# An expert layer whose order is planned by a list scheduler in the source: every instruction pinned, products chained in PSUM, output sums in DRAM

## The chip, the cores and the metric

One core of a Trainium2 chip runs the whole kernel. The metric is device time in microseconds (us) of one execution, lower is better; three executions of the kernel before were timed. Engine names are those of the profile: PE multiplies matrices and PEld loads its weights beside it, DVE, ACT and POOL work on elements, SP issues most DMAs.

## What is computed

Block-sparse attention (batch 4, 8 heads, 768 positions, head size 64) gives x, 3072 rows of 512. A gate x @ w_gate (8 experts) is turned into weights P by eight rounds of row and column normalisation. Every expert then works on every row, with no routing:

```python
for e in range(E):                    # E = 8, D = 512, F = 1024
    h = np.maximum(x @ w1[e], 0.0)
    ye = h @ w2[e]
    out += P[:, e:e + 1] * ye
```

Both products are large and dense: the expert part is 32 pairs of (expert, batch of 768 rows).

## The kernel before

**Two parts.** The attention part is planned in steps T (`at`, L270): the loop at L927 sorts the work of each step and hands it to `in_order` (L917), which chains every instruction to the one made before it on the same engine, so each engine keeps the source's order. Its last steps hold: the values of the last tile (T = 194), the preparation of expert 0's w2 (`start_w2`, L897: a 2 MB load, eight ACT parts at L108, DVE `whole` at L194, a PE transpose `spread` at L114, DVE `power`), and `turn_x` (L793, T = 196 and 197: PE transposes at L798, ACT copies at L805). The expert part that follows isn't chained to it: its instructions are placed by the framework's own scheduler, which may put them before attention instructions made earlier; only side work is held behind its place (`not_earlier`, L983).

**Expert part.** For i = 4e + b, `stage1` (L1199) computes h = relu(x @ w1) and `stage2` (L1312) h @ w2. Each operand is a high and a low fp16 half, so one term takes three matmuls. Both stages use seven products of half-size blocks in place of eight (p = 0 to 6). Stage one has four quarters `qi` per i. A quarter's product (L1208) is six matmuls of 384 columns into one PSUM bank of its own; bank by bank, DVE adds it to running sums in SBUF (`comb`, L1220, seven per quarter), ACT copies the first (L1255), applies relu (L1259, L1275, L1279, L1287) and writes the high half of h (L1230); the low half is a subtraction on POOL for p = 2, 3, 5 and on DVE for the rest (L1234, L1240). POOL makes four sums (L1282, L1094). Stage two has seven products by three row blocks `ci`; each group is twelve matmuls of 256 columns (L1333), read by DVE into `acc` (L1357), for expert 0 in part by ACT (L1354). The output sums `acc` of all four batches stay in SBUF; the last expert's are stored at L1363, one row block and half at a time. While i is in stage two, i + 1 is in stage one: the main loop alternates products of the one with quarters of the other.

**Side work.** New weights of each expert pass once through one raw buffer: load (L177), eight ACT parts (L108), splits into halves on ACT (L1072) and DVE (L1076), block sums on POOL (L1087). A `Slots` queue (L996) with hand-set costs and due times spreads this over the main loop. Expert 0's splits, the last batch's x (`finish_x`, L346) and the gate's rounds (`balance`, L1152) fall into the first rounds of the expert part. x is loaded per product, in 384 KB pieces (L227).

Of the kernel before, what the change touches and what calls it, by code (L numbers as in the profile page):

```python
# [24 lines left out]
TOP = 2.0 ** 12  # L25
# [4 lines left out]
HDOWN = 2.0 ** -20  # L30
HUP = 2.0 ** 20
# [9 lines left out]
PRE, LB2, LB1 = 0, 1, 1  # L41
PIN = 0
TW = 100
TF = 146
HQ = 300
NHA = 10
LATE = 40
# [3 lines left out]
LAV = 3  # L51


@with_exitstack
def tile_sparse_attention_moe(
# [79 lines left out]
    def scale_power(tag, s, inv):  # L135
# [6 lines left out]
        nc.vector.tensor_scalar(s, s, TOP, None, ALU.mult)  # L142
        nc.vector.tensor_scalar(inv, a, 1.0 / TOP, None, ALU.mult)

# [35 lines left out]
    def scale_steps(which, e, vector=nc.vector, scalar=nc.scalar):  # L180
# [18 lines left out]
        def power():  # L199
            vector.tensor_reduce(out=a, in_=wr["all", which], axis=AX.X, op=ALU.max)  # L200
            vector.tensor_scalar(a, a, TINY, HUGE, ALU.max, ALU.min)
            ai = a.bitcast(I32)
            vector.tensor_scalar(ai, ai, 0x7F800000, None, ALU.bitwise_and)
            vector.reciprocal(s, a)
            vector.tensor_scalar(s, s, TOP, None, ALU.mult)
            vector.tensor_scalar(inv, a, 1.0 / TOP, None, ALU.mult)

# [138 lines left out]
    def finish_x(b):  # L346
        xf = xfs.pop(b).rearrange("p k c t -> p k (c t)")
        quad = {
            (j, k): xf[:, j * KH : (j + 1) * KH, k * TH : (k + 1) * TH]
            for j in range(2) for k in range(2)  # L350
        }

        def split(src, p, nm):
            st = xst.tile([P, 2, KH, TH], F16, tag="xs", name=f"xs_{b}_{nm}")
            nc.scalar.activation(st[:, 0], src, AF.Copy)
            nc.vector.tensor_tensor(out=st[:, 1], in0=src, in1=st[:, 0], op=ALU.subtract)
            if p is not None:
                nc.sync.dma_start(out=xd[b][:, p], in_=st)
            return st

        def plain(k):
            sts = [
                split(quad[j, k], {(0, 0): 0, (1, 0): 1, (1, 1): 2}.get((j, k)), f"b{j}{k}")
                for j in range(2)
            ]
            ps = bank[0](f"lg_{b}_{k}")
            for i in range(CH):
                for kc in range(KD):
                    for m, (l, w) in enumerate(((1, gh), (0, gl), (0, gh))):
                        nc.tensor.matmul(  # L370
                            ps[:, i * NE : (i + 1) * NE],
                            lhsT=sts[kc // KH][:, l, kc % KH, i * P : (i + 1) * P],
                            rhs=w[:, kc],
                            start=(kc == 0 and m == 0), stop=(kc == KD - 1 and m == 2),
                        )
            t0 = b * NC + k * CH
            nc.vector.tensor_scalar(
                lg[:, t0 : t0 + CH].rearrange("p t e -> p (t e)"), ps[:, : CH * NE],
                inv_v[:, b : b + 1], inv_g, ALU.mult, ALU.mult,
            )  # L380

        def diff(nm, x, y, out, p):
            nc.gpsimd.tensor_tensor(out=out, in0=x, in1=y, op=ALU.subtract)
            split(out, p, nm)

        x00, x01, x10, x11 = (quad[j, k] for j in range(2) for k in range(2))
        return [
            lambda: plain(0),
            lambda: plain(1),
            lambda: diff("t1", x01, x00, x00, 4),  # L390
            lambda: diff("t3", x11, x01, x01, 6),
            lambda: diff("t2", x11, x00, x00, 5),
            lambda: diff("t4", x10, x00, x10, 3),
        ]

    with ExitStack() as actx:
# [18 lines left out]
        plan = xfp.tile([P, 2, S], BF16, tag="xf", name="plan")  # L415
        onehot = plan[:, 0]
# [148 lines left out]
        def scale_v(b):  # L565
            sv[b] = small.tile([P, 1], F32, tag="sv", name=f"sv_{b}")
            scale_power(f"v{b}", sv[b], inv_v[:, b : b + 1])
# [246 lines left out]
        def split_gate():  # L814
            scale_power("g", sg, inv_g)
# [116 lines left out]
        xlast = finish_x(B - 1)  # L932

    class InOrder:
        def __init__(self, engine):
            self.engine = engine

        def __getattr__(self, name):
            call = getattr(self.engine, name)
            if not PIN:  # L940
                return call
            return lambda *a, **kw: tc.keep_in_program_order(call(*a, **kw))

    class Pinned:
        vector, scalar, gpsimd = (InOrder(x) for x in (nc.vector, nc.scalar, nc.gpsimd))
# [3 lines left out]
    )  # L949
    sk = mpool("sk", 1)  # L950
    upool = mpool("upool", NU)
    hA = mpool("hA", 1)
    hB = mpool("hB", 1)
    big = mpool("big", 1)
    def spare(n):
        return sk.tile([P, n], F32, name=f"spare_{next(count)}")

    count = iter(range(99))
    ps_h = mpool("ps_h", 4, space=PSUM)
    ps_y = mpool("ps_y", 4, space=PSUM)  # L960

    DH = DM // 2
    w2p = [big.tile([P, 2, KF // 2, DH], F16, name=f"w2p_{p}") for p in range(NP)]
    hfree = [
        (hA if n < NHA else hB).tile([P, 2, TH], F16, name=f"h_{n}") for n in range(NHT)
    ]
    accs = {b: big.tile([P, NC, DM], F32, name=f"acc_{b}") for b in range(B // 2)}
    bank[0] = lambda nm: ps_y.tile([P, 512], F32, tag="py", name=nm)
    spread_bank[0] = lambda nm: ps_h.tile([P, 512], F32, tag="ph", name=nm)

    def acc(t):
        return accs[t // NC][:, t % NC]

    def finish_late():
        slots.need(("late", 0, 0))
        late.close()
        right = mpool("right", 1, side="right")
        for b in range(B // 2, B):
            accs[b] = right.tile([P, NC, DM], F32, name=f"acc_{b}")

    aside = set()

    def not_earlier(fn):  # L983
        made = nc.cur_bb.bb.instructions
        n = len(made)
        fn()
        for ins in list(made[n:]):
            if ins.engine not in SIDE:
                continue
            for old in reversed(made[:n]):  # L990
                if old.engine == ins.engine and old.name not in aside:
                    tc.add_manual_dep(ins, old.name, behind, reason="not_ahead_of_its_place")
                    break
            aside.add(ins.name)

    class Slots:  # L996
        def __init__(self):
            self.now, self.pe, self.busy = 0, 0.0, [0.0, 0.0, 0.0]
            self.urgent, self.lazy = [], []
            self.last = 0  # L1000

        def add(self, fn, key, delay=1, lazy=False, dve=0.0, act=0.0, pool=0.0, gap=0):
            queue = self.lazy if lazy else self.urgent
            queue.append((fn, key, self.now + delay, (dve, act, pool), gap))

        def charge(self, costs):
            self.busy = [x + c for x, c in zip(self.busy, costs)]

        def run(self, queue, n):
            fn, key, _, costs, _ = queue.pop(n)  # L1010
            self.charge(costs)
            if queue is self.lazy:
                self.last = self.now
            if key[0] in ("scale", "w1", "w2"):
                not_earlier(fn)
            else:
                fn()

        def fits(self, costs):
            return all(  # L1020
                not c or x <= self.pe + lead
                for x, c, lead in zip(self.busy, costs, LEADS)
            )

        def tick(self, pe, dve, act=0.0):
            self.now += 1
            self.pe += pe
            self.busy = [max(x, self.pe - lag) for x, lag in zip(self.busy, LAGS)]
            self.charge((dve, act, 0.0))
            n, held = 0, set()  # L1030
            while n < len(self.urgent):
                _, key, ready, costs, _ = self.urgent[n]
                if key not in held and ready <= self.now and self.fits(costs):
                    self.run(self.urgent, n)
                    n, held = 0, set()
                    continue
                held.add(key)
                if key[0][0] == "sum":
# [358 lines left out]
    for i in range(NI):  # L1397
# [35 lines left out]
        if last:  # L1433
            parts[1]()
# [43 lines left out]
```

## Time and profile before

| | |
|---|---|
| three executions | 2235.66, 2236.8 (median), 2239.47 us |
| profiled execution, first to last instruction (span) | 2232.8 us |
| PE busy | 2162.7 us, 97% |
| DVE, ACT, POOL busy | 75%, 58%, 63% |
| first expert matmul | 414.07 us into the span |

The span is of one more execution than the three; its own time outside the span is not listed, so the span is read beside the median, which is 4.0 us longer. "Busy" of PE is the union of matmul rows whose ends are modelled, so a busy PE need not be a PE at its full rate; the rate is read from how many matmuls a stretch holds.

### The profile page before, as it was taken

What the parts mean: (1) busy time and instruction counts of PE and PEld (TensorE: products, weight loads), DVE (VectorE), ACT (ScalarE), POOL (GpSimd) and SP (SyncE); (2) the same over time, 40 slices, a digit from 0 to 9 for tenths busy, and PEclk for the clock granted to TensorE, in tenths of its full rate; (3) what the DMA queues carried; (4) which work ended last, traced back from release to release, by engine and by line L of the source; (5) the groups of instructions that cost most, each with busy time, mean ns of one, the idle gap of its engine ahead of it and who ended that gap; (6) DMA issues with size and microseconds to landing.
All of it is one profiled execution on the core that took longest, in us unless ns stands there. A gap on an engine that the chain in (4) does not pass through costs nothing.

```text
span 2232.8 us, 47313 instructions
## 1 busy us (share of the span) xinstructions
PE 2162.7 (97%) x18892; PEld 1596.3 (71%) x18892; DVE 1671.7 (75%) x2927; ACT 1285.1 (58%) x2393; POOL 1412.6 (63%) x1481
## 2 busy tenths in 40 slices
PE   6999999889999999999999999999999999999999
PEld 4777766566777777777777777777677767776777
DVE  8888888778778767866786678667866786678664
ACT  5788888754566546554555455545554555455442
POOL 5556678685568555855685658565856585658553
PEclk9999999999999999999999999999999999999999
DMA  7766965312121212121212121212121212121221
GB/s 167 151 154 138 209 146 126 130 69 88 51 88 50 88 50 88 50 89 50 88 50 88 50 88 50 89 50 88 50 88 50 88 51 88 51 88 58 79 79 51
DMA packets 195347, 192.36 MB, mean 86 GB/s; under 512 B 132125, under 2 KB 150581, under 8 KB 195125
## 3 DMA queue, kind: packets, MB, share of 16 engines
q1 hardware_dynamic: 194560, 189.30, 29.3%
q8 instruction: 148, 2.42, 0.5%
q14 instruction: 75, 0.61, 0.1%
q10 hardware_dynamic: 564, 0.03, 0.0%
HBM read 140.54 MB, written 17.30 MB: 71 GB/s over the span
## 4 chain that ended last, share of the span: by engine, by line
PE 64%; DVE 11%; POOL 9%; ACT 7%; issue 4%; DMA 4%; DVEq 0%; SPq 0%; POOLq 0%; ACTq 0%
PE py L1333 26%; PE p L1208 25%; PE u L767 3%; DMA r<-in_moe_w_dram 3%; PE m L669 2%; PE m L672 2%; PE t L702 2%; PE t L705 2%; ACT h L1230 2%; POOL r L1087 2%; ACT unread L108 2%; POOL s L1282 2%; POOL h L1240 1%; DVE attic L1076 1%; POOL r L1094 1%
## 5 line engine op out<-in xcount | busy, mean ns | idle before, releaser
L1333 PE MATMUL py<-w2p,h 128*128 128x256 f16 x8064 | 952.4, 273 | 12.2 <-ACT acc L1354 4.2
L1333 PEld LDWEIGHTS <-h 128*128 128x128 f16 x8064 | 787.7, 98 | 154.0 <-issue 16.6
L1240 POOL TENSOR_TENSOR h<-u,h 128x384 f16<-128x384 f32 x128 | 124.4, 972 | 558.8 <-ACT h L1230 541.4
L1208 PEld LDWEIGHTS <-attic 128*128 128x128 f16 x3072 | 299.5, 98 | 202.2 <-issue 20.5
L1208 PE MATMUL p<-attic 128*128 128x384 f16 x2304 | 412.0, 326 | 12.7 <-DVE a L1220 8.0
L1208 PE MATMUL p<-arena 128*128 128x384 f16 x2304 | 415.3, 326 | 5.9 <-DVE u L1220 2.7
L1357 DVE SCALAR_TENSOR_TENSOR acc<-py,spare,acc 128x256 f32<-128x256 f32 (+1 forms) x588 | 295.0, 514 | 145.3 <-PE py L1333 143.2
L1208 PEld LDWEIGHTS <-arena 128*128 128x128 f16 x2304 | 225.2, 98 | 134.1 <-issue 7.8
L1230 ACT ACTIVATE h<-c 128x384 f16<-128x384 f32 x256 | 132.5, 520 | 319.9 <-DVE c L1220 263.0
L1220 DVE SCALAR_TENSOR_TENSOR a<-p,a 128x384 f32<-128x384 f32 x384 | 211.2, 550 | 22.7 <-PE p L1208 16.6
L678 DVE TENSOR_REDUCE top<-m 128x1 f32<-128x768 f32 x192 | 181.7, 951 | 46.7 <-PE m L672 45.8
L710 ACT ACTIVATE pe<-t,qk 128x768 int32<-128x768 f32 x192 | 172.3, 899 | 68.7 <-PE t L705 60.3
L1230 ACT ACTIVATE h<-s 128x384 f16<-128x384 f32 x128 | 66.8, 522 | 174.3 <-POOL s L1282 174.2
L1230 ACT ACTIVATE h<-r 128x384 f16<-128x384 f32 x256 | 131.3, 519 | 61.3 <-POOL r L1094 58.3
L1240 DVE TENSOR_TENSOR h<-s,h 128x384 f16<-128x384 f32 x128 | 106.2, 830 | 79.5 <-ACT h L1230 79.3
L1094 POOL TENSOR_TENSOR r<-s,r 128x384 f32<-128x384 f32 x128 | 153.6, 1200 | 10.0
L1094 POOL TENSOR_TENSOR c<-c,r 128x384 f32<-128x384 f32 x128 | 151.1, 1180 | 10.0
L1282 POOL TENSOR_TENSOR s<-a,u 128x384 f32<-128x384 f32 x128 | 140.9, 1101 | 17.3 <-ACT a L1279 17.1
L1208 PE MATMUL p<-arena,attic 128*128 128x384 f16 x768 | 146.2, 326 | 5.4 <-ACT a L1255 4.7
L1240 POOL TENSOR_TENSOR h<-r,h 128x384 f16<-128x384 f32 x128 | 133.9, 1046 | 18.3 <-ACT h L1230 15.2
L724 POOL TENSOR_SCALAR pl<-pe 128x768 f16<-128x768 uint16 x112 | 96.3, 864 | 70.9 <-ACT pe L710 68.8
L1087 POOL TENSOR_TENSOR r<-r 128x256 f32<-128x256 f32 (+1 forms) x106 | 119.0, 1148 | 31.0 <-DVE arena L1076 31.0
(206 smaller groups left out, 3717.3 us busy)
## 6 DMA issues: line engine op xcount, KB each, us to landing
arena<-xd SPq DMA_DIRECT2D x128, 384.0 KB, 3.9
attic<-xd SPq DMA_DIRECT2D x96, 384.0 KB, 4.2
r<-in_moe_w_dram SPq DMA_DIRECT2D x16, 2048.0 KB, 8.7
arena<-in_q_dram SPq DMA_DIRECT2D x16, 384.0 KB, 4.3
arena<-in_k_dram SPq DMA_DIRECT2D x16, 384.0 KB, 4.7
arena<-in_v_dram SPq DMA_DIRECT2D x4, 1536.0 KB, 7.8
xd<-xs_t SPq DMA_DIRECT2D x16, 384.0 KB, 2.9
out_dram<-acc SPq DMA_DIRECT2D x48, 128.0 KB, 1.7
```

The lines of the kernel that those rows point to most:

```text
L678: nc.vector.tensor_reduce(out=tops[n][:, c : c + 1], in_=sc[:, :S], axis=AX.X, op=ALU.max)
L710: nc.scalar.activation(pe, sc[:, :S], AF.Exp, bias=EXP_SHIFT, scale=qk[n // 2][3])
L724: nc.gpsimd.tensor_scalar(lo, low, FINE, 1.0, ALU.mult, ALU.mult)
L1087: lambda c=c: Pinned.gpsimd.tensor_tensor(out=out[:, c], in0=x[:, c], in1=y[:, c], op=op),
L1094: nc.gpsimd.tensor_tensor(out=out, in0=x, in1=y, op=ALU.subtract)
L1208: nc.tensor.matmul(ps, lhsT=w1p[p][:, l, kc, fs], rhs=xp[p][:, r, kc], start=(kc == 0 and m == 0), stop=(kc == KH - 1 and m == 2),)
L1220: nc.vector.scalar_tensor_tensor(out=t, in0=ps, scalar=HDOWN, in1=other, op0=ALU.mult, op1=ALU.add)
L1230: nc.scalar.activation(h[:, 0], src, AF.Relu if relu else AF.Copy)
L1240: eng.tensor_tensor(out=h[:, 1], in0=src, in1=h[:, 0], op=ALU.subtract)
L1282: nc.gpsimd.tensor_tensor(out=s1, in0=a1, in1=u3, op=ALU.add)
L1333: nc.tensor.matmul(py, lhsT=hs[i, p, kc][:, l, tsl], rhs=w2p[p][:, r, kc], start=(old is None and kc == 0 and m == 0), stop=(kc == KF // 2 ...
L1357: nc.vector.scalar_tensor_tensor(out=dst, in0=src, scalar=c, in1=dst, op0=ALU.mult, op1=ALU.add)
```

## The change

The expert part is rewritten. Each operation becomes a `Job` with its engine, a cost in us written in the source, its dependencies and the buffers that it takes and gives back. `Plan.run` lists the jobs by a simulation in the source: PE takes, of the jobs that are ready, the one planned earliest; DVE, ACT and POOL take the one with the earliest due time; times other than PE's are raised by 6%, and 0.2 us lies between engines. The resulting order goes through `in_order`, so it is chained on every engine, behind the attention part.

Stage one now works on two quarters at a time. Products 0, 5, 4, 2 add up in one PSUM bank per quarter and 6, 3 in another; between two products of a chain the running sum is read out (ACT three times and once more with relu, DVE three times per quarter). The low halves of p = 0, 2, 3, 4, 5, 6 go to DVE or POOL, whichever the plan finds free sooner. The output sums live in DRAM between experts (`accd`): two pieces of 768 KB per i are loaded and stored, through three buffers in SBUF; the last expert stores four pieces of 384 KB per i to the output. x pieces, weights and their splits are the same work, ordered by the plan. With `TWO = ()` the code for a second level of block products is present but makes no instruction. The scale constants change by powers of two. Matmul shapes and counts of both stages are unchanged.

```diff
 EPS = 1e-9
-NHT = 30
-NU = 8
-LOP = (2, 3)
-LOPE = (2, 3, 5)
-NLE = 99
-LEADS, LAGS = (1.0, 1.0, 1.0), (1.0, 1.0, 1.0)
-SD = (2, 3, 4, 5)
+TWO = ()
+NB1, NH, NPAIRS, NU, NACC = 4, 28, 8, 8, 3
+SLK, SLK2, SHIFT, EASE = 1.5, 2.0, 8.0, 0.3
...
+class Plan:
+    LAT = 0.2
+    DMA_RATE, DMA_LAND = 190.0, 2.0
+    MARGIN = 1.06
...
+                    if e == "PE":
+                        best = min(ok, key=lambda j: (j.pt is not None, j.pt if j.pt is not None else j.seq))
+                    else:
+                        for j in sorted(ok, key=lambda j: (j.dl, j.seq)):
...
+                    start(best, e, t)
...
+    def order(self):
+        for j in self.done:
+            def fn(j=j):
+                self.current = j.eng
+                j.fn()
+            yield fn
...
-        xlast = finish_x(B - 1)
...
-    ps_h = mpool("ps_h", 4, space=PSUM)
-    ps_y = mpool("ps_y", 4, space=PSUM)
...
-    hfree = [
-        (hA if n < NHA else hB).tile([P, 2, TH], F16, name=f"h_{n}") for n in range(NHT)
+    ps = mpool("ps", 1, space=PSUM)
+    w2p = [big.tile([P, 2, h2, DH], F16, name=f"w2p_{p}") for p in range(NP)]
+    shelf = {
+        "s1": [ps.tile([P, 512], F32, name=f"p_{n}") for n in range(NB1)],
+        "s2": [ps.tile([P, 512], F32, name=f"y_{n}") for n in range(8 - NB1)],
+        "acc": [big.tile([P, CH, DM], F32, name=f"acc_{n}") for n in range(NACC)],
+    }
+    accd = [
+        [dram.tile([P, CH, DM], F32, name=f"accd_{b}_{j}") for j in range(2)] for b in range(B)
...
+                for q, (j, end) in outer(0, X, True, {}).items():
+                    k0[q] = scaled_copy(cell(R, q), bank(X[q]), (j,), take=first(R, q), dl=end + SLK)
+                for q, (j, end) in outer(1, Z, True, {}).items():
+                    r_[q] = scaled_add(cell(R, q), bank(Z[q]), cell(R, q), (j, k0[q]), drop=(Z[q],), dl=end + SLK)
+                for q, (j, end) in outer(5, X, False, {q: (k0[q],) for q in qis}).items():
+                    k5[q] = scaled_copy(cell(C, q), bank(X[q]), (j,), take=first(C, q), dl=end + SLK)
+                for q, (j, end) in outer(6, Y, True, {}).items():
+                    k6[q] = scaled_copy(cell(U, q), bank(Y[q]), (j,), take=first(U, q), dl=end + SLK)
...
+                for q, (j, end) in outer(3, Y, False, {q: (k6[q],) for q in qis}).items():
+                    c_[q] = scaled_add(cell(C, q), bank(Y[q]), cell(C, q), (j, k5[q]), drop=(Y[q],), dl=end + SLK)
...
+            def low(out_, x, y):
+                if plan.current == "POOL":
+                    nc.gpsimd.tensor_tensor(out=out_, in0=x, in1=y, op=ALU.subtract)
+                else:
+                    nc.vector.scalar_tensor_tensor(
+                        out=out_, in0=x, scalar=1.0, in1=y, op0=ALU.mult, op1=ALU.subtract
+                    )
...
+                    lo = job(
+                        {"DVE": 0.65, "POOL": 1.02},
+                        lambda: low(h.tile[:, 1], src(), h.tile[:, 0]), (hi,), drop=drop,
+                    )
...
+        if e:
+            for j in range(2):
+                ld = plan.dma(
+                    lambda j=j: nc.sync.dma_start(out=pieces[j].tile, in_=accd[b][j]), 768,
+                    (accstore[i - B, j],), take=(pieces[j],),
+                )
...
+        if e < NE - 1:
+            for j in range(2):
+                accstore[i, j] = plan.dma(
+                    lambda j=j: nc.sync.dma_start(out=accd[b][j], in_=pieces[j].tile), 768,
+                    tuple(writes[j]), drop=(pieces[j],),
+                )
...
-    stage1(0, 0)
-    for part in split_w2(0, wr[2]):
-        part()
-    stage1(0, 1)
-    stage1(0, 2)
-    stage1(0, 3)
-    load_x(1)
-    for step in xlast:
-        slots.add(step, ("late", 0, 0), LATE, True, dve=1.0, act=0.8, pool=0.8)
-    balance()
-    queue_weight(0)
+    started = job({"-": 0.0}, lambda: None, ())
+    fetch_w2(0, started)
+    stored, keeps = ascend(B - 1)
+    xstored.update(stored)
+    stage1(0, 0.0, S1A)
+    clock = S1A
+    even = balance(keeps)
+    weight_job(0, (even,))
...
-        stage2(i, 1)
-        stage2(i, 0)
...
-        quarter(0)
-        stage2(i, 5)
-        if last:
-            parts[1]()
-        quarter(1)
...
+        if more:
+            load_x(i + 1)
+        if b == B - 1 and e + 1 < NE:
+            fetch_w1(e + 1)
+        stage2(i, clock + SHIFT, length)
...
+        if more:
+            stage1(i + 1, clock, length)
+        clock += length
+    plan.run()
+    for fn in plan.order():
+        in_order(fn)
...
-    nc = _bacc.Bacc("TRN2", target_bir_lowering=False, num_devices=1)
+    nc = _bacc.Bacc("TRN2", target_bir_lowering=False, num_devices=1, dynamic_dma_scratch_size=1024)
```

## Rows read from the trace of the kernel before

**Rows 1.** The page: busy us (share of the span) and instructions by engine
```profile
PE 2162.7 (97%) x18892; PEld 1596.3 (71%) x18892; DVE 1671.7 (75%) x2927; ACT 1285.1 (58%) x2393; POOL 1412.6 (63%) x1481
```

**Rows 2.** Windows: length, then busy us (instructions) by engine, PE clock, DMA
```profile
414.00:664.00 250.00, 232.57 (x1791) 167.38 (x1788) 194.25 (x354) 145.74 (x309) 157.61 (x146) 1.00 0.22 77
...
664.00:2201.00 1537.00, 1515.01 (x11537) 1126.92 (x11537) 1117.78 (x1987) 813.35 (x1636) 979.66 (x930) 1.00 0.20 69
...
2201.00:2228.30 27.30, 27.29 (x250) 24.17 (x247) 12.90 (x25) 3.96 (x8) 7.05 (x7) 1.00 0.15 49
...
2228.30:2232.80 4.50, 0.00 (x0) 0.00 (x0) 0.48 (x1) 0.00 (x0) 0.00 (x0) 1.00 0.20 62
...
1336.00:1560.00 224.00, 220.71 (x1682) 164.15 (x1682) 164.14 (x292) 117.76 (x239) 144.10 (x137) 1.00 0.20 69
```

**Rows 3.** The chain that ended last: start us, length us, engine, line
```profile
2169.03 2.93 PE p L1208 x18
...
2171.96 7.32 PE py L1333 x67
```

**Rows 4.** Waits of PE from 414 us on: us in total, times, longest
```profile
PE p L1208 <- DVE a L1220: 10.4, 10, 1.3
...
PE p L1208 <- ACT a L1255: 5.9, 6, 1.2
...
PE py L1333 <- DVE acc L1357: 3.5, 9, 0.8
...
PE cs L1177 <- DVE spare L1171: 3.1, 3, 2.2
```

**Rows 5.** Timeline, 406 to 426 us: start, length, engine, line [idle before]
```profile
406.03 0.46 SPq L177 DMA_DIRECT2D r<-in_moe_w_dram  x1
...
413.91 0.56 DVE L720 TENSOR_SCALAR pl<-pe 128x768 f16<-128x768 uint16 x1 [0.65 <-ACT pe L710]
...
414.07 3.09 PE L1208 MATMUL p<-arena 128*128 128x384 f16 x18
...
416.93 0.63 ACT L108 ACTIVATE unread<-r 128x512 bf16<-128x512 f32 x1 [3.06 <-DMA r<-in_moe_w_dram]
...
423.52 0.19 ACT L108 ACTIVATION_READ_ACCUMULATOR unread<-r 128x1 f32 x1
...
424.97 0.27 PE L114 MATMUL u<-ident,ma_w 128*128 128x128 f32 x1
...
425.23 0.97 PE L1208 MATMUL p<-arena,attic 128*128 128x384 f16 x5
```

**Rows 6.** Groups: xcount, busy us, mean ns, idle before; or ns min/median/max
```profile
L1220 DVE SCALAR_TENSOR_TENSOR a<-p,a x384: 537/548/560, 418.7 to 2201.8; 128x384 f32<-128x384 f32 x192
...
L1240 DVE TENSOR_TENSOR h<-r,h x128: 539/608/1387, 420.9 to 2197.7; 128x384 f16<-128x384 f32 x128
...
L1240 DVE TENSOR_TENSOR h<-a,h x128: 543/954/1352, 429.8 to 2205.9; 128x384 f16<-128x384 f32 x128
...
L1255 ACT ACTIVATE a<-p 128x384 f32<-128x384 f32 x128 | 61.4, 480 | 45.1 <-PE p L1208 44.2
...
L1076 DVE SCALAR_TENSOR_TENSOR w2p<-r,sw,w2p 128x1024 f16<-128x1024 f32 x48 | 66.1, 1378 | 12.9 <-ACT w2p L1072 12.9
```

**Rows 7.** The page, DMA issues: xcount, KB each, us to landing
```profile
r<-in_moe_w_dram SPq DMA_DIRECT2D x16, 2048.0 KB, 8.7
...
xd<-xs_t SPq DMA_DIRECT2D x16, 384.0 KB, 2.9
...
out_dram<-acc SPq DMA_DIRECT2D x48, 128.0 KB, 1.7
```

**Rows 8.** The clock: a window, and matmuls of one shape around it
```profile
28.00:30.10 2.10, 2.10 (x8) 0.89 (x7) 2.10 (x4) 0.00 (x0) 0.75 (x1) 0.50 1.37 164
...
29.03 0.63 PE L669 MATMUL m<-kt,qt 128*128 128x512 f16 x1
...
31.87 0.38 PE L669 MATMUL m<-kt,qt 128*128 128x512 f16 x1
```

More of the change, by code (lines that the diff above doesn't have):

```diff
@@ L344, in plan_x @@
             at(T + 3, FIRST, x_store, b, nm, p)
[L346 to L394, printed above, removed]
     with ExitStack() as actx:
@@ L981, in tile_sparse_attention_moe @@
[L981 to L1038, printed above, removed]
-                    held.update((("h", key[1], p),) + key[1:] for p in (2, 4, 5, 6))
-                n += 1
-            while self.lazy and self.due(self.lazy[0]):
-                self.run(self.lazy, 0)
-        def due(self, item):
-            _, _, ready, costs, gap = item
-            return max(ready, self.last + gap) <= self.now and self.fits(costs)
-        def settle(self, i, qi):
-            while any(x[1][1:] <= (i, qi) for x in self.urgent):
-                self.run(self.urgent, 0)
-        def need(self, key):
-            for queue in (self.urgent, self.lazy):
-                while any(x[1] == key or x[1][0] == key for x in queue):
-                    self.run(queue, 0)
@@ L1139, in first, with split @@
-        def first():
-            one(0, m[0, 0])
-            queue_sum(m[0, 0], m[1, 1], t1, ("w2", e, 5))
-            one(1, m[1, 0])
-            queue_sum(m[1, 0], m[1, 0], m[0, 0], ("w2", e, 3))
+        stored = {}
+        def split(src, p, deps):
+            st = hold("xs")
+            hi = job({"ACT": 0.83}, lambda: nc.scalar.activation(st.tile[:, 0], src, AF.Copy), deps, take=(st,))
+            lo = job(
+                {"DVE": 1.3},
+                lambda: nc.vector.tensor_tensor(out=st.tile[:, 1], in0=src, in1=st.tile[:, 0], op=ALU.subtract),
+                (hi,),
+            )
+            if p is not None:
+                stored[p] = plan.dma(
+                    lambda: nc.sync.dma_start(out=xd[b][:, p], in_=st.tile), 384, (lo,), drop=(st,)
+                )
+            return st, lo
@@ new lines, in ascend @@
+        los, keeps = {}, []
+        for k in range(2):
+            ls, keep = plain(k)
+            keeps.append(keep)
+            for j in range(2):
+                los[j, k] = ls[j]
+        last = None
+        lows = [los[j, k] for j in range(2) for k in range(2)]
+        for x, y, o, p in (
+            ((0, 1), (0, 0), (0, 0), 4), ((1, 1), (0, 1), (0, 1), 6),
+            ((1, 1), (0, 0), (0, 0), 5), ((1, 0), (0, 0), (1, 0), 3),
+        ):
+            d = job(
+                {"POOL": 2.05},
+                lambda o=o, x=x, y=y: nc.gpsimd.tensor_tensor(
+                    out=quad[o], in0=quad[x], in1=quad[y], op=ALU.subtract
+                ),
+                lows,
+            )
+            _, lo = split(quad[o], p, (d,))
+            lows = lows + [d, lo]
@@ new lines, in tile_sparse_attention_moe, with raw_load, scale_jobs, make @@
+    scaled, split_done, used1, used2 = {}, {}, {}, {}
+    last_s3 = [()]
+    raw_free = [()]
+    pwe = {}
+    def raw_load(which, e):
+        return plan.dma(lambda: load_w(which, e), 2048, raw_free[0])
+    def scale_jobs(which, e, loaded):
+        cell = {}
+        def make():
+            cell["steps"] = scale_steps(which, e)
+        parts = []
+        last = job({"-": 0.0}, make, (loaded,))
+        for k in range(8):
+            last = job({"ACT": 0.81}, lambda k=k: cell["steps"][0][k](), (last,))
+            parts.append(last)
+        whole = job({"DVE": 0.16}, lambda: cell["steps"][1](), parts)
+        bk = hold("s1", ordered=False)
+        def spread():
+            spread_bank[0] = lambda nm: bk.tile
+            cell["steps"][2]()
+        pe = job({"PE": 0.3}, spread, (whole,), take=(bk,))
+        power = job({"DVE": 1.2}, lambda: cell["steps"][3](), (pe,), drop=(bk,), rush=True)
+        scaled[which, e] = power
+        return parts, power
@@ new lines, in split_jobs @@
+    def split_jobs(which, e, dst, src, deps):
+        s = lambda: wr["s", which]
+        hi = job(
+            {"ACT": 1.14}, lambda: nc.scalar.activation(dst[:, 0], src(), AF.Copy, scale=s()),
+            tuple(deps) + (scaled[which, e],),
+        )
+        lo = job(
+            {"DVE": 1.5},
+            lambda: nc.vector.scalar_tensor_tensor(
+                out=dst[:, 1], in0=src(), scalar=s(), in1=dst[:, 0], op0=ALU.mult, op1=ALU.subtract
+            ),
+            (hi,),
+        )
+        return [hi, lo]
@@ new lines, in scaled_add, with scaled_copy @@
+    def scaled_add(out_, bank_, add, deps, drop=(), dl=None):
+        return job(
+            {"DVE": 0.56},
+            lambda: nc.vector.scalar_tensor_tensor(
+                out=out_(), in0=bank_(), scalar=HDOWN, in1=add(), op0=ALU.mult, op1=ALU.add
+            ),
+            deps, drop=drop, dl=dl,
+        )
+    def scaled_copy(out_, bank_, deps, take=(), drop=(), dl=None, relu=False):
+        return job(
+            {"ACT": 0.49},
+            lambda: nc.scalar.activation(out_(), bank_(), AF.Relu if relu else AF.Copy, scale=HDOWN),
+            deps, take=take, drop=drop, dl=dl,
+        )
@@ L1433, in tile_sparse_attention_moe @@
[L1433 to L1447 removed]
+        s1 = (S1A if (i + 1) // B == 0 else S1B) if more else 0.0
+        length = S2 + s1
+        if TWO and i < B:
+            prep_x(i)
+            late_users += [xprep[i, p] for p in TWO]
```

1163 lines of the change are left out of this document (818 added, 345 removed).

## The prediction

> **What bounds the kernel now.** I read the page first: PE is busy for 97% of the span, every other engine for 75% or less [rows 1]. A busy share of PE doesn't show its rate, so next the chain that ended last: 18 matmuls of stage one take 2.93 us and 67 of stage two 7.32 us [rows 3], which is 0.1628 and 0.1093 us each. The expert part has 5376 and 8064 of them: 875.1 + 881.0 = 1756.1 us that no order can shorten, since shapes and counts stay.
>
> Then the windows, for what lies above this floor. The first expert matmul starts at 414.07 [rows 5] and the last ends near 2228.3, so the part lasts 1814.2 us, 58.1 above the floor. PE idles for 250 - 232.6 = 17.4 us of it in the first 250 us and for 1537 - 1515.0 = 22.0 after that, 39.4 in all [rows 2]; in one later expert it is 224 - 220.7 = 3.3. The other 18.7 are small PE work (transposes, the gate's matmuls, the end of attention) and gaps too short for the view. After the last matmul come 4.5 us of end. The waits view names what PE waited for: mostly DVE sums of stage one, then an ACT copy, sums of stage two and the gate's rounds [rows 4]. So 39.4 us, 1.8% of the time, is all that a better order can win in the expert part, and what the change loses elsewhere counts against it.
>
> The span is 2232.8; the median of the runs is 4.0 above. I sum against the span and add 4.0.
>
> **The start, a loss.** The first expert matmuls now sit in a gap of attention. The load of expert 0's w2 is issued at 406.03, its first part runs on ACT at 416.93 and the eighth ends at 423.7; the transpose that follows on PE stands at 424.97 [rows 5]. Meanwhile PE works on stage one from 414.07 on. Expert work is now chained on every engine behind the whole attention plan, so PE must first do that transpose and two sets of x transposes behind it. Without three foreign ACT instructions among the parts they end about 0.8 us sooner, at 422.9; a reduction, the transpose, a reduction, and twice transposes and a copy follow, about 2.5 us by transposes of 0.27 us [rows 5] and copies of 0.48 [rows 6]. First expert matmul: 425.4, 11.3 us later. Bounds: 0 if the hoisting goes on, 15 if SP or ACT are late as well. The wait is at the end of a 10.9 us load, and queued behind it are all PE work, and on ACT the copies of x.
>
> PE then stands from about 415.2 (the last pl ends at 414.5 [rows 5], its value matmuls are short) to 423.2. After a pause of 1.6 us at 26 us the granted clock was 0.50, the 1.2 GHz level, for 3.4 us, and a 512-column matmul took 0.63 us in place of 0.38 [rows 8]. I add 2.0 us, half of about 4 at the lower level; bounds 0 and 3.4.
>
> **Stage one.** Per quarter, DVE's sums from PSUM fall from seven to three: 128 quarters x 4 x 0.55 us [rows 6] = 282 us less DVE time. ACT has four reads where it had one copy and a relu: 128 x 2 x 0.48 [rows 6] = 123 us more. In a cycle of 224 us DVE goes from 164 to about 129 us, ACT from 118 to about 133 [rows 2]: both far from full, so this is worth only what the waits behind them were. New waits: products 5, 4, 3 and 2 go into a bank only after it was read. A read is 0.48 to 0.55 us [rows 6] and two groups of the pair, 6 x 0.1628 = 0.98 us each, lie between, with groups of stage two besides; that is the cover. If it goes (a 1.38 us weight split [rows 6] just ahead on the reading engine), up to about 1 us is lost, with all later PE work queued behind, as PE's order is fixed.
>
> **The order.** In the old queue, weight splits and sums meet on DVE and PE pays 3.3 us per expert. The plan puts the read with the nearest due time first and holds back a long job that would hit one. Its costs are those of the rows: 0.978 and 1.312 us per group are 6 x 0.163 and 12 x 0.109; 0.56 and 0.49 us for the reads. So its order should hold on the chip where durations are steady. I take 1 us per expert for seven experts, 7 us, and 6 for the first rounds, where w2's splits, the last x and the gate's rounds crowd DVE, ACT and POOL: 13 us. Bounds: 0, and 39.4 as before.
>
> **Sums in DRAM.** Experts 0 to 6 store 56 pieces, experts 1 to 7 load 56, each 768 KB: 88 MB over 1800 us, some 49 GB/s on top of 69 to 77 at a DMA share of 0.2 [rows 2]. No row has a 768 KB piece; 384 KB land in 2.9 us and 2048 KB in 8.7 [rows 7]; I take 5, nearer the smaller. Three buffers serve two pieces in use, so a load starts when the last round's piece is stored and has half a round, some 25 us, until its first sum. Inside the kernel I cost it at nothing. Without that cover, 56 x 2.9 = 162 to 56 x 8.7 = 487 us would show; a gain I exclude, as DRAM replaces no transfer. SP issues four more DMAs per 55 us round, 0.46 us each by the weight load's issue [rows 5], among x loads that wait for PE anyway. At the end a 384 KB store replaces 128 KB ones: 2.9 - 1.7 = 1.2 us [rows 7], bounds 0 and 2.5.
>
> **Nothing for the rest**: powers of two in the scales, fewer h buffers (28, one round's worth), a smaller scratch for descriptors (the page's DMAs go through hardware queues), the code that `TWO = ()` leaves out. Small PE work falls from 18.7 to 16.5, as 2 us of attention now lie ahead of the start.
>
> **The sum**: 425.4 + 2.0 + 1756.1 + 16.5 + 13 + 5.7 = 2218.7 of span, with 4.0 around it 2222.7 us, so 2223. Against before: -26.4 idle, +13.3 start, -2.2, +1.2.
>
> **Rivals.**
> *DVE and POOL collide and the pinned order passes it on.* Low halves subtract two SBUF operands on DVE: 0.54 us at best, 0.61 or 0.95 in the median, up to 1.39, while sums with one operand from PSUM stay within 0.537 to 0.560 [rows 6]. The plan books 0.69. A read of PSUM queued behind a late one is 0.3 to 0.7 us late. It decides when PE loses 0.6 us more per round than forecast (18.6 us over 31 rounds); at 1.5 us per round the idle time is 46, the time 2256. For: PE can't reorder now. Against: reads have due times 1.5 us off and DVE is 58% full.
> A milder form: the sums taken away are those that never collide (0.537 to 0.560), the subtractions that do collide remain, and half of the old waits stay with them. Idle 20 us in place of 13, 2230; I give this 0.15 of the forecast's own 0.50, and its time lies inside that range. The Trainium skill (SBUF — State Buffer, Who interferes with whom) says that a DVE instruction with two SBUF inputs and a GpSimd instruction that reads SBUF exclude each other for a whole instruction, while one with a single SBUF input is free of it. By that rule, the trace agrees.
> *Nothing ever waits.* Idle time near 0: 2210. For it the calibrated costs, against it the first rounds.
> *The start isn't moved.* If the chain doesn't hold expert work back, 13.3 us come back: 2209. Against: the chain already keeps attention's order.
> *Part of the waits stay*, idle 23 to 32 us: 2233 to 2241.
>
> **Chances.** About 0.2%, 4.5 us, is what a measurement here can tell from no change: 2232.3 to 2241.3. Forecast (2213 to 2232) 0.50; nothing waits 0.13; start not moved 0.05; waits stay in part 0.12; collision 0.20. So faster 0.68, same 0.12, slower 0.20. The likeliest case's own range is 2213 to 2232; reaching to the rivals on both sides, with a tenth left out at either end, gives 2208 to 2246.
>
> **What would show it.** Right: the first expert matmul near 425 with a hole in PE from 415 and a window at clock 0.5 behind it; about 1 us idle per expert; three DVE sums per quarter at 0.55; piece loads that nobody waits for. Wrong: PE waits spread evenly over all rounds with DVE low halves at 0.9 or more ahead of them; waits of DVE for pieces from DRAM; expert matmuls still at 414.

## The result, and the profile after

The changed kernel takes 2196.5 us (median of four, 2195.06 to 2197.99), the kernel before on the same chip 2238.1 (2235.66 to 2240.28): ratio 0.981, interval 0.980 to 0.983. Forecast were 2223 us and 2208 to 2246. The sign was right, the gain about three times the forecast one. The profiled execution's span is 2193.6 us, against 2232.8.

The page, busy us by engine, beside [rows 1]:

```profile
PE 2151.1 (98%) x18892; PEld 1599.7 (73%) x18892; DVE 1555.6 (71%) x2485; ACT 1374.3 (63%) x2649; POOL 1388.2 (63%) x1411
```

The windows of the changed kernel, columns as in [rows 2]: the hole at the start, the first rounds, the steady part, one expert, the end, and the stretch at the lower clock:

```profile
417.00:426.57 9.57, 2.07 (x7) 1.32 (x8) 1.14 (x7) 6.27 (x17) 5.50 (x8) 0.65 0.01 4
426.57:664.00 237.43, 235.98 (x1806) 171.53 (x1805) 185.25 (x289) 160.46 (x344) 155.31 (x133) 0.99 0.33 105
664.00:2162.00 1498.00, 1498.00 (x11489) 1124.35 (x11488) 1008.54 (x1601) 884.22 (x1843) 955.44 (x868) 1.00 0.38 124
1336.00:1560.00 224.00, 224.00 (x1720) 168.15 (x1718) 151.41 (x239) 131.53 (x276) 146.33 (x132) 1.00 0.40 131
2189.60:2193.60 4.00, 0.00 (x0) 0.00 (x0) 0.48 (x1) 0.00 (x0) 0.00 (x0) 1.00 0.28 98
419.88:430.12 10.24, 5.62 (x19) 2.96 (x20) 2.96 (x9) 6.18 (x15) 2.95 (x5) 0.50 0.02 9
```

From 664 us on PE has no idle time that the view shows. The same 224 us that held 1682 matmuls [rows 2] hold 1720. All waits of PE from 417 us to the end (us in total, times, longest), beside [rows 4]:

```profile
PE u L335 <- DVE ma_w L415: 7.7, 1, 7.7
PE p L1229 <- DVE spare L1226: 1.1, 1, 1.1
PE u L970 <- ACT xf L977: 0.6, 1, 0.6
PE u L970 <- DVE ma_w L421: 0.4, 1, 0.4
```

Three of the four stand ahead of the first expert matmul; only the 1.1 us, the first product of the gate's rounds, lies in the expert part. The start in the timeline (start, length, [idle before]), beside [rows 5]:

```profile
417.28 0.63 ACT L329 ACTIVATE unread<-r 128x512 bf16<-128x512 f32 x1 [2.83 <-DMA r<-in_moe_w_dram]
...
423.32 0.16 DVE L415 TENSOR_REDUCE ma_w<-mx_w 128x1 f32<-128x8 f32 x1 [6.48 <-ACT unread L329]
...
423.54 0.47 PE L335 MATMUL u<-ident,ma_w 128*128 128x128 f32 x1 [7.72 <-DVE ma_w L415]
...
424.39 0.90 PE L970 MATMUL u<-ident,xn 128*128 128x128 f32 x3 [0.38 <-DVE ma_w L421]
...
425.88 0.90 PE L970 MATMUL u<-ident,xn 128*128 128x128 f32 x3 [0.58 <-ACT xf L977]
...
426.57 0.84 PE L1546 MATMUL p<-arena 128*128 128x384 f16 x2
```

PE waits for the w2 chain as forecast. The page's DMA issues, the new pieces (compare [rows 7]):

```profile
accd<-acc SPq DMA_DIRECT2D x56, 768.0 KB, 3.9
acc<-accd SPq DMA_DIRECT2D x56, 768.0 KB, 4.3
```

**Where the time went.** First expert matmul 414.07 to 426.57: +12.5. From there to the end of the last product 1814.2 to 1763.0: -51.2. After it 4.5 to 4.0: -0.5. Together -39.2, the difference of the spans.

### The profile page after: what moved, and what is told of

Its sections match the earlier page's. It is cut to its first block, busy times and chain, and to the rows that moved or that the text cites. A ratio compares the mean times of both kernels' runs of the same rounds, so it can differ in the third digit from the quotient of the medians.

```text
span 2193.6 us, 46709 instructions
## 1 busy us (share of the span) xinstructions
PE 2151.1 (98%) x18892; PEld 1599.7 (73%) x18892; DVE 1555.6 (71%) x2485; ACT 1374.3 (63%) x2649; POOL 1388.2 (63%) x1411
## 4 chain that ended last, share of the span: by engine, by line
PE 91%; DVE 4%; POOL 2%; ACT 1%; DMA 1%; issue 1%; SPq 0%; ACTq 0%; POOLq 0%
PE y L1866 39%; PE p L1546 38%; PE u L939 4%; PE m L841 2%; PE t L874 2%; PE m L844 2%; PE t L877 2%; DVE top L850 1%; POOL u L1784 1%; POOL pair L1784 1%; DMA r<-in_moe_w_dram 0%; PE u L970 0%; DMA qt<-qs 0%; ACT unread L329 0%; DVE pl L892 0%
## 5 line engine op out<-in xcount | busy, mean ns | idle before, releaser
L1866 PE MATMUL y<-w2p,h 128*128 128x256 f16 x8064 | 986.5, 273 | 0.0
L1902 DVE SCALAR_TENSOR_TENSOR acc<-y,spare,acc 128x256 f32<-128x256 f32 (+1 forms) x588 | 305.5, 520 | 314.1 <-PE y L1866 310.6
L1750 POOL TENSOR_TENSOR h<-pair,h 128x384 f16<-128x384 f32 x265 | 271.5, 1033 | 378.6 <-ACT h L1761 363.5
L1784 POOL TENSOR_TENSOR u<-u,pair 128x384 f32<-128x384 f32 x256 | 294.4, 1153 | 210.6 <-ACT u L1528 201.2
L1761 ACT ACTIVATE h<-pair 128x384 f16<-128x384 f32 x640 | 310.1, 516 | 120.7 <-DVE pair L1519 56.0
L1519 DVE SCALAR_TENSOR_TENSOR pair<-p,pair 128x384 f32<-128x384 f32 x384 | 213.5, 556 | 164.8 <-PE p L1546 153.7
L1528 ACT ACTIVATE pair<-p 128x384 f32<-128x384 f32 x384 | 180.9, 488 | 203.1 <-PE p L1546 199.5
L1746 ACT ACTIVATE pair<-pair 128x384 f32<-128x384 f32 x384 | 197.4, 518 | 172.9 <-DVE pair L1519 165.9
L1752 DVE SCALAR_TENSOR_TENSOR h<-u,h 128x384 f16<-128x384 f32 x207 | 192.9, 949 | 26.5 <-ACT h L1761 26.3
L1752 DVE SCALAR_TENSOR_TENSOR h<-pair,h 128x384 f16<-128x384 f32 x247 | 198.3, 827 | 14.4 <-ACT h L1761 14.2
```

Source lines behind the costliest of these rows:

```text
L1519: lambda: nc.vector.scalar_tensor_tensor(out=out_(), in0=bank_(), scalar=HDOWN, in1=add(), op0=ALU.mult, op1=ALU.add),
L1528: lambda: nc.scalar.activation(out_(), bank_(), AF.Relu if relu else AF.Copy, scale=HDOWN),
L1746: return job({"ACT": 0.52}, lambda: nc.scalar.activation(view(), view(), AF.Relu), dep)
L1750: nc.gpsimd.tensor_tensor(out=out_, in0=x, in1=y, op=ALU.subtract)
L1752: nc.vector.scalar_tensor_tensor(out=out_, in0=x, scalar=1.0, in1=y, op0=ALU.mult, op1=ALU.subtract)
L1761: lambda: nc.scalar.activation(h.tile[:, 0], src(), AF.Relu if relu else AF.Copy),
```

## Experiments

Every edit is to the changed kernel, and all of them compute the whole layer. Differences are against its 2196.5 us; the median of the kernel before moved by up to 2.8 us from one set of runs to another, so differences under 3 us are read as none, and the differences below move by up to 3 us if they are taken from the ratios. "Excess" is worked out from the start times of all matmul rows of the expert part: the time from one start to the next less 0.163 us in stage one and 0.1093 in stage two. It holds the waits and also what a lower clock costs. It is 48.8 us in the kernel before and 0.3 in the changed one.

### The start

e1: the eight scale parts of expert 0's w2, the transpose and the reductions leave the attention plan and become jobs.

```diff
             load_w(2, 0)
-            parts, whole, spread, power = scale_steps(2, 0)
-            for n, part in enumerate(parts):
-                at(NTILE + n // 4, LATER, part)
...
-            parts = [start]
-            scaled[2, e] = start
+            parts, _ = scale_jobs(2, e, start)
```

> The eight ACT parts, the reduction, the PE transpose and the power steps of expert 0's w2 become jobs of the plan; only the load stays in the attention plan. If the late start is a real cost, the first expert matmul moves from 426.6 us to about 419 (two sets of x transposes stay ahead of it), the window at clock 0.5 (419.9 to 430.1) is gone or ends sooner, and the time falls by 7.6 + 1.8 = 9.4 us, from 2196.5 to 2187 (2185 to 2190). Rival, the first rounds are bound by w2's splits anyway: the hole in PE moves to the first matmuls of stage two, and the time stays at 2195 to 2198.

2188.1 us, ratio 0.979 (0.9775 to 0.9805): 8.4 us less, or some 5 by the ratios. The timeline of this run:

```profile
417.55 0.55 PE L970 MATMUL u<-ident,xn 128*128 128x128 f32 x3 [1.07 <-DVE xn L960]
...
419.06 1.63 PE L1539 MATMUL p<-arena 128*128 128x384 f16 x9
...
420.38 0.62 ACT L329 ACTIVATE unread<-r 128x512 bf16<-128x512 f32 x1
```

The first expert matmul comes at 419.06, 7.5 us sooner and ahead of the scale parts, and no stretch at the lower clock follows it in the expert part. So the wait for w2 cost about the 9.4 us that were expected of it, and it wasn't needed. The other 5 us to the 414.07 of the kernel before stay: the x transposes are still ahead.

### The order

e2 lists ready jobs in source order and holds none back; e3 hands the list to the framework without the chain; e5 does both.

```diff
-                        for j in sorted(ok, key=lambda j: (j.dl, j.seq)):
+                        for j in sorted(ok, key=lambda j: j.seq):
...
-                            if e in ("DVE", "ACT", "POOL"):
+                            if False:
```

> Same jobs, same chains, same pinning; DVE, ACT and POOL take the ready job that stands first in the source in place of the one with the nearest due time, and hold nothing back for it. Theory of the order (due times remove the waits): PE idles 20 to 60 us more, time 2215 to 2255. Rival theory of the load (waits went because the chains took 282 us from DVE): PE stays without waits, 2195 to 2202.

```diff
     for fn in plan.order():
-        in_order(fn)
+        fn()
```

> Same jobs handed over in the same order, but the expert part isn't chained on the engines: the framework's own scheduler may move instructions. Theory of the pinning (the framework's moves made the waits of before): waits return, 2210 to 2235, less about 10 us because expert matmuls again move ahead of the w2 transpose. Rival (the order handed over is kept or does not matter): 2185 to 2198, with the start near 415 in place of 426.6.

> The two runs before (source order in the plan's lists, and no pinning) each cost 22 to 24 us. Theory A, that they are two separate losses of the expert part's first rounds and of the changes of expert: without both the loss adds up, 40 to 50 us over the changed kernel, 2236 to 2248 us, no better than the kernel before. Theory B, that they are the same loss seen twice (a read of PSUM that comes late either way): 20 to 30 us over, 2216 to 2227. The steady part, after 700 us, tells which is at work there: about 2 us of PE waits per 200 us by A, under 1 by B.

e2 2220.5 us (ratio 0.993, 0.9916 to 0.9949), e3 2218.8 (0.9925, 0.991 to 0.9939), e5 2217.5 (0.991, 0.9895 to 0.9925): 24, 22 and 21 us more. The two losses don't add up (theory B), and e5's waits of PE after 700 us are 4.2 us in the view, 0.6 per 200 us. That they are the same waits isn't shown: of e2's excess of 23.1 us, 22.1 lie in the first 200 us, of e3's 21.7 only 11.6. A part of e2's is clock. Its windows after the first expert matmuls:

```profile
436.64:443.46 6.82, 5.66 (x18) 2.60 (x18) 6.82 (x9) 6.36 (x10) 6.82 (x5) 0.50 0.00 0
450.28:453.70 3.42, 3.42 (x13) 1.72 (x12) 1.47 (x4) 2.57 (x6) 1.69 (x2) 0.50 0.99 371
460.52:470.77 10.25, 7.34 (x23) 3.18 (x23) 7.94 (x9) 5.71 (x12) 6.04 (x4) 0.50 0.28 88
```

20.5 us at the lower clock, PE busy for 16.4 of them: some 8 us lost, an estimate, beside the waits that they came with. And e3 shows something about the start. Its timeline:

```profile
423.34 0.47 PE L335 MATMUL u<-ident,ma_w 128*128 128x128 f32 x1 [7.58 <-DVE ma_w L415]
...
426.37 1.49 PE L1546 MATMUL p<-arena 128*128 128x384 f16 x4
```

Without the chain between them the expert work still stands behind the transposes of the attention plan.

### Single parts

e4: every product into a bank of its own, seven DVE sums per quarter.

```diff
-                Z = {q: hold("s1") for q in qis}
-                Y = {q: hold("s1") for q in qis}
+                V = {p: X if p == 0 else {q: hold("s1") for q in qis} for p in PORDER}
...
+                product(5, (oA, oA, none))
+                product(6, (oU, oA, lambda q: first(U, q)))
+                product(3, (oC, oU, lambda q: first(C, q)))
+                product(4, (oU, oU, none), (oA, oA, none))
```

> Stage one as before: every product in a PSUM bank of its own, seven DVE sums per quarter and one ACT copy and a relu, 282 us more of DVE and 123 us less of ACT; list scheduler, pinning and sums in DRAM stay. Theory of the load: waits return in the rounds with weight splits, 15 to 35 us, time 2212 to 2232. Theory of the order: DVE goes to about 84% of a round and the plan still finds a place for each read, 2196 to 2202.

2198.4 us, ratio 0.983 (0.9819 to 0.9848). Its page has DVE back above the load of before:

```profile
PE 2154.3 (98%) x18892; PEld 1601.2 (73%) x18892; DVE 1708.4 (78%) x2839; ACT 1271.6 (58%) x2393; POOL 1526.8 (70%) x1569
```

The planned order carries 150 us more of DVE work at no price that can be told.

e6: PE's planned order in runs of four groups of stage one, up to 24 matmuls as in the kernel before.

```diff
+        many = [0, t0]
...
-            j = job({"PE": dur}, fn, deps, take=take, pt=at[0], stream="1")
+            if many[0] % 4 == 0:
+                many[1] = at[0]
+            many[0] += 1
+            j = job({"PE": dur}, fn, deps, take=take, pt=many[1], stream="1")
```

> Only PE's planned order is coarser: four groups of stage one in a row (24 matmuls, 3.9 us), as the kernel before has them, in place of one or two. Theory of the interleaving, by which before's waits came from bursts of sums that DVE and ACT can't follow: the waits at the changes of expert come back, 3 to 4 us each, and the time is 2218 to 2230. Order theory, by which the due times alone keep PE fed: the reads still end inside the stage-two work between bursts, 2196 to 2203.

e7: the low halves where they were.

```diff
-                        {"DVE": 0.65, "POOL": 1.02},
+                        {"POOL": 1.02} if p in (2, 3, 5) else {"DVE": 0.65},
```

> The low halves stand where the kernel before has them: products 2, 3, 5 on POOL, the rest on DVE. Placement theory (the plan's free choice is what takes the waits away): 5 to 15 us slower than the changed kernel, 2201 to 2212, with PE waiting for DVE. Order theory: DVE has room either way, within 2 us of it, 2195 to 2199.

e10: `rush=True` on both jobs of `split_jobs`, so weight splits run ahead of everything.

```diff
-            tuple(deps) + (scaled[which, e],),
+            tuple(deps) + (scaled[which, e],), rush=True,
...
-            (hi,),
+            (hi,), rush=True,
```

> The weight splits (ACT 1.14, DVE 1.5 us each) run ahead of anything else as soon as they are ready; all else of the plan stays. Collision theory, by which the kernel before lost its 3 to 5 us per change of expert because splits stood ahead of PSUM reads: PE's waits come back at the changes of expert, 25 to 50 us in all, 2220 to 2245. Cover theory (the chains and the finer order of PE give enough cover for one late read): under 8 us, 2197 to 2204.

e11: two buffers for the output sums.

```diff
-NB1, NH, NPAIRS, NU, NACC = 4, 28, 8, 8, 3
+NB1, NH, NPAIRS, NU, NACC = 4, 28, 8, 8, 2
```

> Two buffers for the output sums in place of three: a piece is loaded only when the one before it has been stored. With the 3.9 and 4.3 us that a load and a store of 768 KB take, theory A (stage two's first sums wait for it and PE with them): 28 rounds x 2 pieces x 2 to 6 us each less what the second stage's other banks cover, 2220 to 2400. Theory B (the plan moves other work ahead): 2196 to 2205.

e6 2197.2 (ratio 0.982, 0.9803 to 0.9836), e7 2195.5 (0.981, 0.9795 to 0.9824), e10 2200.4 (0.984, 0.9821 to 0.9853), e11 2198.0 (0.983, 0.981 to 0.9842). Only e10's 4 us is more than the 3 us that are read as none, and its interval still overlaps that of the changed kernel. So no single one of these parts carries the gain, the collision of splits with reads among them, and the DRAM sums are covered even with a third less buffer.

### The plan's costs

e12: durations of DVE, ACT and POOL times 0.6 and no time between engines. e16: times 0.8. e15: times 1.0.

```diff
-    LAT = 0.2
+    LAT = 0.0
...
-    MARGIN = 1.06
+    MARGIN = 0.6
```

> The plan's costs are made wrong: durations of DVE, ACT and POOL times 0.6 in place of 1.06, no time between engines. Theory of calibration (the order holds because the costs are those of the chip): the pinned order puts readers where they come late, as much as source order costs or more, 2215 to 2260. Theory of due times (their order alone matters, costs little): 2196 to 2206.

> The same times a fifth too short (0.80). With e12 at 105 us for 0.60 and no time between engines: a loss in proportion to the error would be some 40 us, 2225 to 2245; if the 0.2 us between engines covers it, 2198 to 2210.

> The plan's times of DVE, ACT and POOL times 1.00 in place of 1.06. If calibration with spare is needed (durations vary: low halves took 0.83 to 0.95 us where the plan has 0.69), 2200 to 2210; if right costs alone are enough, 2195 to 2199.

e12 2301.8 us (ratio 1.029, 1.0275 to 1.0311), e16 2248.3 (1.005, 1.0039 to 1.0069), e15 2215.5 (0.991, 0.9889 to 0.9922): 105, 52 and 19 us more. Waits of PE in e12 from 427 us on:

```profile
PE p L335 <- DVE ma_w L415: 35.5, 13, 3.3
PE p L1250 <- DVE spare L1244: 15.7, 5, 6.3
PE p L1546 <- ACT pair L1528: 14.4, 15, 2.0
```

The pinned order puts a weight's transpose where the plan thinks that its eight ACT parts have ended; they haven't, and all of PE stands for 2.7 us on average. In e15 it is mostly the gate's chain. Here it is on PE, with what runs on DVE in the meantime:

```profile
467.81 1.14 PE L1546 MATMUL p<-arena,attic 128*128 128x384 f16 x6
467.49 5.87 DVE L1752 SCALAR_TENSOR_TENSOR h<-u,h 128x384 f16<-128x384 f32 x5
473.29 0.34 DVE L1226 TENSOR_REDUCE spare<-lg 128x1 f32<-128x192 f32 x1
473.68 0.48 PE L1229 MATMUL p<-ident,spare 128*128 128x128 f32 x1 [4.73 <-DVE spare L1226]
```

The gate's reduction (L1226), for which PE waits, stands behind five low halves that take some 1.17 us each, where the source writes 0.65. 18.7 of e15's 19.4 us of excess lie in the first 200 us; after 640 us the view shows only 3.2 us of waits. The spare of 6% is worth 19 us, nearly all of it there. In all three runs a part of the loss is clock: behind the first expert matmuls' stretch come two more at 0.50 in e15, eight in e16 and fourteen in e12, 10, 31 and 58 us in all. Half of PE's busy time in them, an estimate, is 5, 14 and 26 us of the loss. What the 0.2 us between engines are worth alone was not tried.

### Several parts together

e13 is e4's edit with e5's two, e14 these and e7's.

> Own banks and seven DVE sums per quarter (e4, 2 us alone), with source order and no pinning (e5, 21 us). Load theory, by which DVE's room is what a bad order lives on: much more than the sum of the two, 2230 to 2245. Additive: 2197 + 2 + 21 = 2220, within 4 us.

> As e13, and the low halves of products 2, 3, 5 on POOL, the rest on DVE as the kernel before has them. Load theory: as e13 or up to 10 us more, 2230 to 2255, the expert part near the 1814 us of the kernel before. Additive: within 3 us of e13, both near 2220.

e13 2227.9 us (ratio 0.996, 0.9945 to 0.9975), e14 2242.0 (1.0027, 1.0017 to 1.0038): 31 and 45 us more. By addition they would be 23 and 22. The chains are worth 2 us in the planned order and 10 without it, the placement of the low halves nothing and 14. e14's excess is 40.4 us, and its expert part takes 1808.8 us, so these four edits bring back 45.8 of the 51.2 us, a few of them by the clock (6.83 us at 0.50 from 437.87 on, where the kernel before has none). What the other 5.4 us are was not tried. The same expert as in [rows 2], and PE's waits from 426 us on, in e14:

```profile
1336.00:1560.00 224.00, 220.73 (x1685) 164.62 (x1684) 168.15 (x291) 117.69 (x239) 147.35 (x136) 1.00 0.38 125
```

```profile
PE p L1546 <- DVE pair L1738: 11.5, 21, 1.1
PE p L1546 <- ACT u L1735: 5.9, 11, 0.6
```

That is the window of the kernel before, 1682 matmuls and 220.71 us, and the same two waits ahead, stage one's sums on DVE and its ACT copy [rows 4].

### A faster kernel

With PE full, only less PE work helps. e8 takes three of stage one's products apart once more.

```diff
-TWO = ()
+TWO = (1, 3, 6)
```

> TWO = (1, 3, 6) for experts 1 to 7: three of stage one's products are taken apart once more, 21 groups of 6 matmuls of 192 columns in place of 12 groups of 6 of 384. PE theory (PE is full, only its work counts): if a 192-column matmul starts every 0.082 us, half of the 0.163 of 384 columns, 28 rounds save 12 x 0.978 - 21 x 0.49 = 1.45 us each, 40 us in all, 2157 us, and at 0.098 us a matmul, should the weight load be what limits it, 2196 - 28 x (11.74 - 12.35), 2213. Rival: the sums of the second level fill DVE and POOL, and waits eat the gain: 2180 to 2200.

2199.1 us (ratio 0.9825, 0.9811 to 0.984): no gain. The floor fell: its 192-column matmuls start 0.082 us apart, so the three shapes need 1717.7 us. But the excess rose to 41 us, 25 of them between 528 and 728 us, where the second level's x is made beside expert 0's side work; some 5 of these, an estimate, are clock (13.65 us at 0.50, PE busy for 10.9). e9 therefore starts the second level at expert 2, makes its x in expert 1, and takes e1's start:

```diff
-        two = TWO if e else ()
+        two = TWO if e > 1 else ()
...
-        if TWO and i < B:
+        if TWO and B <= i < 2 * B:
...
```

> Start jobs in the plan (2188.1 us alone) and the second level of products only for experts 2 to 7, its x pieces made during expert 1. In e8 a 192-column matmul took 0.082 us, so a round saves 72 x 0.1628 - 126 x 0.082 = 1.39 us, 24 rounds 33.4: 2154.7 us if PE stays fed. Theory that e8's lost 25 us (527 to 727 us) come from the making of the second level's x on top of expert 0's side work: 2155 to 2165. Rival, that the second level itself fills DVE and POOL: the losses move to expert 1 and stay, 2175 to 2190.

2180.2 us (2177.04 to 2181.91), ratio 0.975 (0.973 to 0.9764): faster than both kernels, 16 us ahead of the changed one and 8 ahead of e1, but 25 above the sum for a full PE. Its waits of PE from 416 us on:

```profile
PE p L1568 <- DVE u L1610: 5.0, 8, 1.1
PE p L1568 <- ACT u L1521: 3.9, 5, 1.4
PE p L1568 <- DVE pair L1648: 3.9, 5, 1.6
```

The second level's groups (L1568) wait for reads of their own chains, in nearly every expert: 23 us of excess in all. The crowd of e8 is gone (3.8 us of excess between 528 and 728 us). For the rest the rival holds in so far as the waits come with the second level, though not in expert 1, where it looked for them. A group of the second level lasts half as long, which would halve the cover of a read; that this is the cause was not tried.

## Why the prediction was wrong

**The start** was right: +11.3 forecast, +12.5 measured; the parts ended at 423.3 (422.9 forecast), and the 2.5 us behind them were 3.3. Its reason was not: the chain isn't what moved it, since e3 without it starts at 426.37. What costs 7.5 us of it is that PE's transpose for w2 stands in the attention plan (e1). Why the framework could pass it in the kernel before was not tried.

**The clock** was right in size: the lower level lasts to 430.12, 3.55 us into the expert part, 1.8 us lost (2.0 forecast).

**The floor**, 1756.1 us, held: PE runs at it.

**The failed step is the idle time**: "I take 1 us per expert for seven experts, 7 us, and 6 for the first rounds ... 13 us". The view shows 1.1, and none in the steady part. The rival "nothing ever waits" had the mechanism, with a chance of 0.13. What the runs showed in its place: with the costs as the source has them, even without spare, the plan leaves PE 3.2 us of waits after 640 us (e15), so the 1 us per expert, for which no row was given, wasn't there. In the first rounds it is the 6% of spare that takes most of the waits away: without it the excess there is 18.7 us in place of 3.7, and the longest wait lies behind low halves that outlast their written cost. Neither steadier sums nor the due times alone carry it: with costs a fifth too short the same rules lose 52 us (e16). The prediction weighed single costs and didn't weigh the spare.

**A second term was misread**: "The other 18.7 are small PE work ... and gaps too short for the view", of which 16.5 were kept. Besides products, clock and idle only 1763.0 - 1756.1 - 1.8 - 1.1 = 4.0 are left. Most of the 18.7 were waits. A matmul's row lasts longer than the time to the next start (0.326 us against 0.163 in stage one, 0.273 against 0.109 in stage two), so each wait hides its first 0.16 us under the row before. In the kernel before, on PE:

```profile
1385.03 0.71 PE L1333 MATMUL py<-w2p,h 128*128 128x256 f16 x5 [0.32 <-DVE acc L1357]
1387.08 0.65 PE L1208 MATMUL p<-attic 128*128 128x384 f16 x3 [1.34 <-DVE a L1220]
```

and on DVE:

```profile
1382.56 2.02 DVE L1076 SCALAR_TENSOR_TENSOR w2p<-t,sw,w2p 128x1024 f16<-128x1024 f32 x1
...
1384.90 0.87 DVE L1240 TENSOR_TENSOR h<-r,h 128x384 f16<-128x384 f32 x1
...
1386.48 0.54 DVE L1220 SCALAR_TENSOR_TENSOR a<-p,a 128x384 f32<-128x384 f32 x1
```

Five stage-two matmuls from 1385.03 on, 0.109 us apart, were due to be followed at 1385.58; the next starts at 1387.08, so 1.50 us are lost where the view says 1.34. (On DVE a weight split of 2.02 us, a sum of stage two and a subtraction of 0.87 us run ahead, and the sum that PE waits for comes only at 1386.48.) Counted from start to start, 84 waits over 0.1 us make 52.1 us, not 39.4: the upper end of what an order could win was itself too low by 12.7 us. The two errors together (11.9 and 12.5 us), a start 1.2 later and an end 1.7 shorter make the 25 us by which the span missed its sum.

**Stage one's chains** were costed at the waits behind them, and that is so in a good order (e4); that they matter in a bad one (e13) was not seen. **Sums in DRAM** cost nothing, as forecast; a piece takes 3.9 or 4.3 us, not 5, and e11 shows the cover has room. **The end** took 4.0 us, not 5.7.

**The collision rival** had its mechanism and not its price. Two groups of the changed kernel, ns min/median/max:

```profile
L1519 DVE SCALAR_TENSOR_TENSOR pair<-p,pair x384: 540/558/560, 431.5 to 2153.6; 128x384 f32<-128x384 f32 x192
```

```profile
L1752 DVE SCALAR_TENSOR_TENSOR h<-pair,h x247: 543/605/2167, 441.7 to 2166.6; 128x384 f16<-128x384 f32 x124
L1752 DVE SCALAR_TENSOR_TENSOR h<-u,h x207: 545/924/2106, 449.3 to 2165.4; 128x384 f16<-128x384 f32 x104
```

Subtractions of two SBUF operands take up to four times their shortest, sums with one PSUM operand stay within 540 to 560 ns. Of these 454 subtractions, the 259 over 700 ns have POOL work beside them for 95% of their time on average, the 157 under 570 ns for 30%. By the Trainium skill (SBUF — State Buffer, Who interferes with whom), a DVE instruction with two SBUF inputs contends with a GpSimd instruction that reads SBUF; the trace agrees. PE pays little for them in the changed kernel, and e7's other placement changes nothing; that this is because reads are ordered ahead is argued, not shown. But its one wait in the expert part is of this kind, on DVE:

```profile
490.25 2.90 DVE L1752 SCALAR_TENSOR_TENSOR h<-pair,h 128x384 f16<-128x384 f32 x2
493.07 0.34 DVE L1226 TENSOR_REDUCE spare<-lg 128x1 f32<-128x192 f32 x1
```

And without the spare it is the longest wait of e15 (4.73 us, above).

## What to carry to other kernels

Count the waits of a pipelined engine from start to start against the stride of its shape, not from the gaps of its busy rows. An order pinned from a simulation lives on its costs: too short by 20% cost 52 us here, as written and without spare 19, and 6% over left 1.1 us of waits, so measure the durations first, those that vary above all, and then add spare for long chains of short instructions that end on the bounding engine, as the gate's here. Count with a wait what the lower clock behind it costs, by the estimates about a quarter of the loss in three of these runs. And undo parts of a change together as well as one by one: chains and placement, not told from none alone, were worth 24 us once the order was gone.

## What was not expected of the hardware

The granted clock fell to 0.50, the 1.2 GHz level, not only at the start: in e2 three more stretches came among the first products, the last two at waits of 3.3 and 3.6 us; they cost some 8 us beside some 15 us of waits. It stayed at 0.50 for 10.24 us in the changed kernel (the window above, PE busy 5.62 us of it), where a shorter pause had brought 3.4 us [rows 8]. The length is not set by the pause alone: the same pause of 1.60 us at 26 us, in the same attention work, was followed by 3.41 us at 0.50 in the kernel before, 6.83 us in e1 and none in the changed kernel. Matmuls of 192 columns, each with a weight load whose row lasts 0.098 us, started every 0.082 us in e8: the load was no limit.
